# Hash attention and squared-ReLU feed-forward on one core: hash products in array quarters, key bits by Sign on ACT, one reciprocal spread by a matmul

## The chip, the core and the metric

The kernel runs on one core of a Trainium2 chip. The metric is device time in microseconds (us), the median of the runs shown. The engines are PE (TensorE), DVE (VectorE), ACT (ScalarE), POOL (GpSimd) and SP (SyncE, which issues DMAs). Each takes its instructions in program order.

## The reference, cut

```
q, k, v: (4, 8, 768, 64)   proj: (64, 6)   w_in: (512, 2048)   w_out: (2048, 512)

q_bucket = sum over 6 bits of (q @ proj > 0) * 2^bit          # k_bucket likewise
scores   = q @ k^T / 8, set to -1e9 where q_bucket != k_bucket
attn     = exp(scores - max) / (sum + 1e-9)
x        = (attn @ v), heads side by side: (3072, 512)
h        = x @ w_in ;  r = max(h, 0) ;  out = (r * r) @ w_out
```

## The kernel before, in words

**First stage, attention.** Heads are handled in 16 pairs (`pr`), two heads on the 128 partitions, 64 each. A pair has 768 queries and 768 keys, and is walked in six steps (`kt`), one for each 128 keys. The loop runs over `u`, the number of the step over all pairs, and an engine's instructions stand in the order in which the loop writes them.

- `features(pr, w, r)` (w = 0 queries, 1 keys; r = half of the 768): three PE transposes into a PSUM bank `tp` (L232), copied by ACT to `feat` (L237).
- `hash_bits(pr, w, r)`: one product of 384 columns with `projs[w]`, a 128x128 matrix holding `proj` for both heads (L244, tile `hp`), and one DVE instruction that makes of it the numbers `bits` in bf16 (L247): compare with `bars`, multiply by `gains`. Query bits and key bits are made such that their product is zero where all six bits agree and hugely negative elsewhere.
- `score(pr, kt)`: bits product and feature product of both heads add up in PSUM tiles `st` (L274). The two tiles of a step take four banks, and there are no others: a step's score waits for the exp of the step before. ACT then makes `e` = exp of it (L281), one instruction for each head.
- `attend(pr, kt)`: `e` times `v` into tile `xo` (L306), two steps behind the score. There is one `xo`: the first attend of a pair waits until the pair before has been normalized.
- `add_up(pr, kt)`: DVE adds the `e` of the step into `total` (L295), one step behind the score.
- `sum_up(pr)`: once a pair, `total` summed over keys by four PE products with ones (L320, tile `tot`), a DVE transpose (`flip`), one small addition (`once`), eight reciprocals of 32 partitions that copy the result to where both halves of the queries need it (`rec`, L336), and a DVE transpose that spreads it (`recs`, L340). `normalize(pr)` multiplies `xo` by `recs` into `x_t` (L350).
- `PREPARE` says which parts of the next pair's features and bits are made in which step.
- The weights come as 64-bit floats and are turned into 32-bit ones beside the attention, 32 pieces, one every third step (`load_weight`, `part_weight`, `round_weight`). For a piece DVE cuts out exponent and mantissa (L127, L131), POOL scales the exponent (L136, L139), ACT makes `one` of the mantissa (L142); a step later DVE rounds (L152, L156) and POOL multiplies (L159). Two pieces fall on a pair: `part_weight` at kt 0 and kt 3, `round_weight` at kt 1 and kt 4.

In a step of the loop before, the order is: score, the totals of a pair that is done, attend, normalize, PREPARE, add_up, weights.

**Second stage, feed-forward.** Six chunks of 512 tokens: `hid` (L453), ReLU on ACT, square on DVE, `y` (L470), out.

PSUM has eight banks: four for `st`, two for `xo`, two that `tp`, `hp` and `tot` take in turn (`bank`).

Of the kernel before, what the change touches and what calls it, by code (L numbers as in the profile page):

```python
# [33 lines left out]
def kernel(  # L34
# [131 lines left out]

    projs, bars, gains = [], [], []
    for w, name in ((0, "q"), (1, "k")):  # L170
        projs.append(const.tile([P, P], FP32, name=f"proj_{name}"))
        bars.append(const.tile([P, 1], FP32, name=f"bar_{name}"))
        gains.append(const.tile([P, 1], FP32, name=f"gain_{name}"))
    pj = const.tile([P, NBITS], FP32, name="pj")
    ones = const.tile([P, 32], FP32, name="ones")
    NRING = 8
    ring = [const.tile([P, S + 1], FP32, name=f"e{i}") for i in range(NRING)]

    def constants():
        N = NBITS  # L180
        for h in range(2):
            r = h * D
            nc.gpsimd.dma_start(out=pj[r:r + D], in_=proj)
        for w in range(2):
            nc.gpsimd.memset(projs[w], 0.0)
            nc.vector.memset(bars[w], 0.0)
            nc.vector.memset(gains[w], float(w == 0))
        for h in range(2):
            r = h * D
            nc.vector.memset(bars[0][r:r + 2 * N], -1.0)  # L190
            nc.vector.memset(bars[0][r:r + N], 0.0)
            nc.vector.memset(bars[1][r:r + N], -1.0)
            nc.vector.memset(gains[1][r:r + 3 * N], 2.0 * FAR)
            nc.vector.memset(gains[1][r:r + 2 * N], -FAR)
            for w, at in ((0, 0), (0, 2 * N), (1, N), (1, 2 * N)):
                nc.vector.tensor_copy(
                    out=projs[w][r:r + D, r + at:r + at + N], in_=pj[r:r + D]
                )
        nc.vector.memset(ones, 1.0)
        for e in ring:  # L200
            nc.vector.memset(e[:, S:S + 1], TINY)

# [33 lines left out]
            )  # L236
        nc.scalar.copy(out=feat[pr, w][:, r * HS:(r + 1) * HS], in_=tp[:, 0:HS])  # L237

    def hash_bits(pr, w, r):
        if r == 0:  # L240
            bits[pr, w] = p_f.tile([P, S], BF16, name=f"bits{w}")
        cut = slice(r * HS, (r + 1) * HS)
        hp = bank("hp")
        nc.tensor.matmul(  # L244
            out=hp[:, 0:HS], lhsT=projs[w], rhs=feat[pr, w][:, cut], start=True, stop=True
        )
        nc.vector.tensor_scalar(  # L247
            out=bits[pr, w][:, cut], in0=hp[:, 0:HS], scalar1=bars[w], scalar2=gains[w],
            op0=ALU.is_gt, op1=ALU.mult,
        )  # L250


    PREPARE = (
        ((features, 0, 0), (features, 0, 1)),
        ((features, 1, 0),),
        ((features, 1, 1), (hash_bits, 0, 0)),
        ((hash_bits, 0, 1),),
        ((hash_bits, 1, 0),),
        ((hash_bits, 1, 1),),
    )  # L260

    weights = {}
# [36 lines left out]
    def attend(pr, kt):  # L299
# [3 lines left out]
        for c in range(2):  # L303
            n = HS + c
            for h in range(2):
# [4 lines left out]
                    start=(kt == 0), stop=(kt == SB - 1),  # L310
                )

    def sum_up(pr):


# [10 lines left out]
        NB = HS // 32  # L326
        once = p_n.tile([P, NB], FP32, name="once")
        nc.vector.tensor_scalar(
            out=once, in0=flip.rearrange("p (n f) -> p n f", f=32)[:, :, 0],
            scalar1=S * TINY, scalar2=None, op0=ALU.add,  # L330
        )
        rec = p_n.tile([P, 2, NB], FP32, name="rec")
        for g in range(4):
            for c in range(2):
                at = 64 * (g // 2) + 32 * c
                nc.vector.reciprocal(  # L336
                    out=rec[g * 32:(g + 1) * 32, c], in_=once[at:at + 32]
                )
        recs[pr] = p_n.tile([P, S], FP32, name="recs")
        nc.vector.transpose(  # L340
            out=recs[pr].rearrange("p (n f) -> p n f", f=32),
            in_=rec.rearrange("p c (n o) -> p (c n) o", o=1).to_broadcast([P, S // 32, 32]),
        )

    def normalize(pr):
# [14 lines left out]
    with tc.manual_schedule():  # L360
# [5 lines left out]
        for w in range(2):  # L366
            for r in range(2):
                features(0, w, r)
            for r in range(2):
                hash_bits(0, w, r)  # L370
# [299 lines left out]
```

## Time and profile before

| | us |
|---|---|
| median of 3 runs | 1123.32 (1123.3 to 1124.17) |
| the profiled execution | 1123.84 |
| its span | 1122.1 |
| PE busy | 1067.4 |
| DVE, ACT, POOL busy | 418.7, 265.2, 88.6 |
| first score (L274) of the loop starts | 14.22 |
| first matmul of the second stage (L453) starts | 455.49 |

The span runs from the first to the last instruction of one profiled execution; its own time lies 1.74 us above it. Granted TensorE clock over the span: 0.998. In the profile a matmul of 32-bit floats leaves two records, one for each pass, so "x2" behind a hash product is one product. A row of the chain of waits shows what the end of the span hung on at that time. "issue" there is time for which the profile shows no releaser.

### The profile page before, as it was taken

To read this page: it belongs to the slowest core of one execution; us is meant where nothing else is said; L and a number is where in the kernel's file an instruction comes from. 1 tells how busy PE (TensorE), PEld (TensorE's weight loads), DVE (VectorE), ACT (ScalarE), POOL (GpSimd) and SP (SyncE) were. 2 spreads that over 40 slices of the span, in tenths; PEclk is the share of its full clock that TensorE was granted. 3 is DMA by queue.
4 is the path that set the end of the run, shared out by engine and by line. 5 is a ranking of instruction groups with operands and counts; after the bars stand their busy time and mean duration, and the time that the engine had idled before them with its cause. 6 is when DMAs were issued, how large, how long until landed. Compare 5 with 4: busy or idle time off the path is not lost.

```text
span 1122.1 us, 9897 instructions
## 1 busy us (share of the span) xinstructions
PE 1067.4 (95%) x3906; PEld 466.6 (42%) x3906; DVE 418.7 (37%) x707; ACT 265.2 (24%) x409; POOL 88.6 (8%) x106
## 2 busy tenths in 40 slices
PE   6999999999999998999999999999999999999998
PEld 3333333333333333444444444444444444444443
DVE  2777777777777778520034103400120012001100
ACT  3444444444444444210011001100110011001100
POOL 0111111111111112100000000000000000000000
PEclk9999999999999999999999999999999999999999
DMA  8233333332222111000042004200000000000000
GB/s 192 67 82 83 83 82 82 83 81 80 81 80 80 52 38 38 1 1 9 19 146 88 9 19 150 85 9 19 9 1 9 19 9 1 19 20 0 1 19 21
DMA packets 65012, 55.24 MB, mean 49 GB/s; under 512 B 51648, under 2 KB 55744, under 8 KB 64960
## 3 DMA queue, kind: packets, MB, share of 16 engines
q1 hardware_dynamic: 63328, 54.14, 16.7%
q8 instruction: 33, 0.54, 0.2%
q10 hardware_dynamic: 1568, 0.39, 0.2%
q14 instruction: 19, 0.16, 0.0%
q0 software_dynamic: 64, 0.00, 0.0%
HBM read 48.24 MB, written 6.29 MB: 49 GB/s over the span
## 4 chain that ended last, share of the span: by engine, by line
PE 89%; DVE 4%; issue 4%; ACT 2%; DMA 0%; SPq 0%; ACTq 0%; DVEq 0%
PE hid L453 29%; PE y L470 29%; PE st L274 13%; PE xo L306 11%; PE hp L244 3%; DVE total L295 2%; PE tp L232 2%; ACT e L281 2%; PE tot L320 1%; DVE power L127 1%; DVE one L131 1%; DMA q_nat<-in_q_dram 0%; DVE bits L247 0%; DVE gate L461 0%; SPq L219 0%
## 5 line engine op out<-in xcount | busy, mean ns | idle before, releaser
L453 PE MATMUL hid<-x_t,w_in 128*128 128x512 f32 x768 | 330.8, 592 | 0.0
L470 PE MATMUL y<-w_out,gate 128*128 128x512 f32 x768 | 330.6, 592 | 0.0
L461 DVE TENSOR_TENSOR gate<-r 128x512 f32<-128x512 f32 x96 | 66.5, 693 | 506.3 <-ACT r L459 504.9
L470 PEld LDWEIGHTS y<-w_out,gate 128*128 128x128 f32 x768 | 145.9, 190 | 183.7 <-issue 183.4
L453 PEld LDWEIGHTS hid<-x_t,w_in 128*128 128x128 f32 x768 | 145.8, 190 | 183.4 <-issue 182.7
L281 ACT ACTIVATE e<-st 128x768 f32<-128x768 f32 x192 | 145.0, 807 | 132.3 <-PE st L274 132.3
L306 PE MATMUL xo<-e,v_nat 128*64 128x384 f32 (+1 forms) x768 | 146.2, 502 | 22.6 <-issue 22.6
L274 PE MATMUL st<-feat,feat 64*128 64x384 f32 x768 | 158.5, 486 | 0.0
L459 ACT ACTIVATE r<-hid 128x512 f32<-128x512 f32 x96 | 57.3, 597 | 275.9 <-PE hid L453 275.9
L295 DVE TENSOR_TENSOR total<-total,e 128x768 f32<-128x768 f32 x128 | 116.9, 965 | 0.0
L306 PEld LDWEIGHTS xo<-e,v_nat 128*64 128x64 f32 x768 | 48.2, 136 | 110.5 <-issue 107.9
L475 ACT COPY o<-y 128x512 f32<-128x512 f32 x24 | 14.1, 586 | 315.7 <-PE y L470 315.7
L274 PE MATMUL st<-bits,bits 64*128 64x384 bf16 x384 | 70.6, 327 | 18.2 <-ACT e L281 18.0
L274 PEld LDWEIGHTS st<-feat,feat 64*128 64x128 f32 x768 | 69.6, 189 | 31.5 <-issue 31.4
L274 PEld LDWEIGHTS <-bits 64*128 64x128 bf16 x384 | 21.0, 93 | 65.2 <-issue 52.8
L247 DVE TENSOR_SCALAR bits<-hp,bar_q,gain_q 128x384 bf16<-128x384 f32 x32 | 21.7, 677 | 60.2 <-PE hp L244 60.2
L237 ACT COPY feat<-tp 128x384 f32<-128x384 f32 x64 | 29.2, 481 | 55.6 <-PE tp L232 55.6
L136 POOL TENSOR_SCALAR power<-power 128x512 uint32<-128x512 uint32 x32 | 23.9, 748 | 211.0 <-DVE power L127 211.0
L142 ACT ACTIVATE one<-one 128x512 f32<-128x512 uint32 x32 | 20.1, 629 | 70.8 <-DVE one L131 70.7
L247 DVE TENSOR_SCALAR bits<-hp,bar_k,gain_k 128x384 bf16<-128x384 f32 x32 | 21.7, 677 | 40.1 <-PE hp L244 40.1
L295 DVE TENSOR_TENSOR total<-e,e 128x768 f32<-128x768 f32 x32 | 30.2, 984 | 0.0
L244 PE MATMUL hp<-feat,proj_k 128*128 128x384 f32 x64 | 28.9, 536 | 0.0
(50 smaller groups left out, 365.1 us busy)
## 6 DMA issues: line engine op xcount, KB each, us to landing
raw<-in_moe_w_in_dram SPq DMA_DIRECT2D x16, 512.0 KB, 4.3
raw<-in_moe_w_out_dram SPq DMA_DIRECT2D x16, 512.0 KB, 3.6
q_nat<-in_q_dram SPq DMA_DIRECT2D x32, 192.0 KB, 4.6
v_nat<-in_v_dram SPq DMA_DIRECT2D x16, 384.0 KB, 3.3
out_dram<-o SPq DMA_DIRECT2D x24, 256.0 KB, 2.0
raw_qk<-in_q_dram SPq DMA_DIRECT2D x8, 768.0 KB, 4.3
raw_qk<-in_k_dram SPq DMA_DIRECT2D x8, 768.0 KB, 4.3
k_nat<-in_k_dram SPq DMA_DIRECT2D x30, 192.0 KB, 4.6
```

Source lines behind the costliest of these rows:

```text
L136: nc.gpsimd.tensor_scalar(out=power, in0=power, scalar1=1151.0, scalar2=896.0, op0=ALU.min, op1=ALU.max,)
L237: nc.scalar.copy(out=feat[pr, w][:, r * HS:(r + 1) * HS], in_=tp[:, 0:HS])
L244: nc.tensor.matmul(out=hp[:, 0:HS], lhsT=projs[w], rhs=feat[pr, w][:, cut], start=True, stop=True)
L247: nc.vector.tensor_scalar(out=bits[pr, w][:, cut], in0=hp[:, 0:HS], scalar1=bars[w], scalar2=gains[w], op0=ALU.is_gt, op1=ALU.mult,)
L274: nc.tensor.matmul(out=st[h][:, c, 0:HS], lhsT=src[pr, 1][rows, key], rhs=src[pr, 0][rows, cut], start=first, stop=not first,)
L281: nc.scalar.activation(out=e[:, 0:S].rearrange("p (c f) -> p c f", c=2), in_=st[h][:, :, 0:HS], func=ACTF.Exp, scale=scale,)
L295: nc.vector.tensor_tensor(out=totals[pr, h], in0=in0, in1=weights[pr, kt, h][:, 0:S], op=ALU.add)
L306: nc.tensor.matmul(out=xo[h * D:(h + 1) * D, c, 0:n], lhsT=nat[pr][2][:, h, kt * D:(kt + 1) * D], rhs=weights[pr, kt, h][:, c * HS:c * HS ...
L453: nc.tensor.matmul(out=hp, lhsT=w_in[:, ft, ff * P:(ff + 1) * P], rhs=x_t[:, ft, i * NCH:(i + 1) * NCH], start=(ft == 0), stop=(ft == NFT ...
L459: nc.scalar.activation(out=r, in_=hp, func=ACTF.Relu)
L461: nc.vector.tensor_tensor(out=g, in0=r, in1=r, op=ALU.mult)
L470: nc.tensor.matmul(out=y, lhsT=gates[ff][:, n * P:(n + 1) * P], rhs=w_out[:, ff], start=(ff == 0), stop=(ff == NFF - 1),)
```

## The change

Parts of it:

1. `hash_bits` makes both halves of a side (w) at once. `projs[w]` is now 64 columns wide. Four products, each 64 rows by 64 columns of the array, take the four combinations of head and half: bank `near` gets half 0 of head 0 (partitions 0 to 63) and of head 1 (64 to 127), bank `far` gets half 1 with the heads swapped.
2. Query bits are made on DVE as before, from `near` in one instruction and from `far` in two of 64 partitions. Key bits are made on ACT with Sign, in the same three parts. `bars`, `gains` and `lifts` (the bias of Sign) hold new numbers, so that a product is still zero only where all bits agree.
3. `sum_up` takes one reciprocal of all partitions. A new function `spread` copies it to its places by two matmuls of 12 columns with the 0/1 matrices `picks` (made by eight POOL copies at the start), into unused columns of `tot`, and DVE transposes from there.
4. `sum_up` runs beside the attend of the last but one step of its pair (kt 0 of the next pair), `spread` a step later.
5. In a step `add_up` now comes first, and PREPARE comes between score and attend. PREPARE has one entry for each step; the first features of the next but one pair are made at kt 5.
6. Ahead of the loop the first pair's bits are made in two `st` tiles.

```diff
-    projs, bars, gains = [], [], []
-    for w, name in ((0, "q"), (1, "k")):
-        projs.append(const.tile([P, P], FP32, name=f"proj_{name}"))
...
+    HUGE, SMALL = 2.0**64, 2.0**-70
+    projs = [const.tile([P, D], FP32, name=f"proj_{name}") for name in "qk"]
...
+    picks = const.tile([P, 2, P], FP32, name="picks")
...
-    def hash_bits(pr, w, r):
...
+    def hash_bits(pr, w, tiles=None):
+        t = p_f.tile([P, S], BF16, name=f"bits{w}")
+        bits[pr, w] = t
+        near, far = tiles or (bank("near"), bank("far"))
+        for c, hp in ((0, near), (1, far)):
+            for h in range(2):
+                rows = slice(h * D, (h + 1) * D)
+                at = (h ^ c) * D
+                nc.tensor.matmul(
+                    out=hp[at:at + D, 0:HS], lhsT=projs[w][rows],
+                    rhs=feat[pr, w][rows, c * HS:(c + 1) * HS], start=True, stop=True,
+                )
+        def turn(out, in_, at):
+            if w == 0:
+                nc.vector.tensor_scalar(
+                    out=out, in0=in_, scalar1=bars[at], scalar2=gains[at],
+                    op0=ALU.is_gt, op1=ALU.mult,
+                )
+            else:
+                nc.scalar.activation(
+                    out=out, in_=in_, func=ACTF.Sign, scale=HUGE, bias=lifts[at]
+                )
+        turn(t[:, 0:HS], near[:, 0:HS], slice(0, P))
+        for h in range(2):
+            at = (h ^ 1) * D
+            turn(t[h * D:(h + 1) * D, HS:S], far[at:at + D, 0:HS], slice(at, at + D))

     PREPARE = (
-        ((features, 0, 0), (features, 0, 1)),
...
+        (1, features, 0, 1),
+        (1, features, 1, 0),
+        (1, features, 1, 1),
+        (1, hash_bits, 0),
+        (1, hash_bits, 1),
+        (2, features, 0, 0),
     )
...
-        rec = p_n.tile([P, 2, NB], FP32, name="rec")
-        for g in range(4):
-            for c in range(2):
-                at = 64 * (g // 2) + 32 * c
-                nc.vector.reciprocal(
-                    out=rec[g * 32:(g + 1) * 32, c], in_=once[at:at + 32]
-                )
+        nc.vector.reciprocal(out=once, in_=once)
+        onces[pr] = once, tot
+
+    def spread(pr):
+        once, tot = onces.pop(pr)
+        rec = tot[:, HS:HS + 2 * NB]
+        for c in range(2):
+            nc.tensor.matmul(
+                out=rec[:, c * NB:(c + 1) * NB], lhsT=picks[:, c], rhs=once, start=True, stop=True
+            )
         recs[pr] = p_n.tile([P, S], FP32, name="recs")
         nc.vector.transpose(...)
...
         for u in range(len(steps) + 2):
+            if 1 <= u <= len(steps):
+                add_up(*steps[u - 1])
             if u < len(steps):
                 pr, kt = steps[u]
                 if kt == 0 and pr + AHEAD < NP:
                     load_pair(pr + AHEAD, nc.sync)
                 score(pr, kt)
             done = steps[u - 2] if u >= 2 else None
+            if done is not None and done[1] == SB - 1:
+                spread(done[0])
+            if u < len(steps):
+                ahead, f, *args = PREPARE[kt]
+                if pr + ahead < NP:
+                    f(pr + ahead, *args)
             if done is not None:
-                if done[1] == SB - 1:
+                if done[1] == SB - 2:
                     sum_up(done[0])
                 attend(*done)
                 if done[1] == SB - 1:
                     normalize(done[0])
-            if u < len(steps) and pr + 1 < NP:
-                for f, w, r in PREPARE[kt]:
-                    f(pr + 1, w, r)
-            if 1 <= u <= len(steps):
-                add_up(*steps[u - 1])
```

How the instructions stand on the engines, in the order of the program. First PE, from a score to the next at kt 3 and kt 4. The first list is before, where a hash product of half a side (`hp`) follows attend:

```order
L274 MATMUL st<-bits_277,bits_329 128x384
L274 MATMUL st<-feat_222,feat_247 128x384 x2
L306 MATMUL xo<-e_101,v_nat 64x384
L306 MATMUL xo<-e_102,v_nat 64x384
L306 MATMUL xo<-e_101,v_nat 64x385
L306 MATMUL xo<-e_102,v_nat 64x385
L244 MATMUL hp<-feat_443,proj_k 128x384
L274 LDWEIGHTS bits_329
```

The second is the changed kernel at kt 3 (L302 is score, L259 hash product, L334 attend):

```order
L302 MATMUL st<-bits_303,bits_340 128x384
L302 MATMUL st<-feat_212,feat_259 128x384 x2
L259 MATMUL near<-feat_371,proj_q 64x384 x2
L259 MATMUL far<-feat_371,proj_q 64x384 x2
L334 MATMUL xo<-e_107,v_nat 64x384
L334 MATMUL xo<-e_108,v_nat 64x384
L334 MATMUL xo<-e_107,v_nat 64x385
L334 MATMUL xo<-e_108,v_nat 64x385
L302 LDWEIGHTS bits_340
```

The hash products moved between score and attend, and four quarters of both halves stand where one half stood.

Then PE at the totals. In the changed kernel they stand at kt 0, between the transposes and the attend of the last but one step:

```order
L302 MATMUL st<-feat_212,feat_259 128x384 x2
L242 MATMUL tp<-ident,q_nat 128x128 x3
L351 MATMUL tot<-total_245,ones 32x384
L351 MATMUL tot<-total_246,ones 32x384
L351 MATMUL tot<-total_245,ones 32x384
L351 MATMUL tot<-total_246,ones 32x384
L334 MATMUL xo<-e_101,v_nat 64x384
```

and the spread a step later, at kt 1:

```order
L302 MATMUL st<-feat_212,feat_259 128x384 x2
L370 MATMUL tot<-once,picks 128x12 x2
L242 MATMUL tp<-ident,k_nat 128x128 x3
L334 MATMUL xo<-e_103,v_nat 64x384
L334 MATMUL xo<-e_104,v_nat 64x384
```

Before, the totals stood at kt 1, ahead of the attend of the last step, and all that follows from them on DVE stood behind them in that same step.

Last DVE from kt 3 to kt 4, before:

```order
L247 TENSOR_SCALAR bits_476<-hp,bar_q,gain_q 128x384
L295 TENSOR_TENSOR total_449<-total_449,e_101 128x768
L295 TENSOR_TENSOR total_450<-total_450,e_102 128x768
L127 TENSOR_SCALAR power<-raw 128x512
L131 TENSOR_SCALAR one<-raw 128x512
L247 TENSOR_SCALAR bits_528<-hp,bar_k,gain_k 128x384
L295 TENSOR_TENSOR total_449<-total_449,e_103 128x768
L295 TENSOR_TENSOR total_450<-total_450,e_104 128x768
L152 SCALAR_TENSOR_TENSOR power<-raw,power 128x512
L156 SCALAR_TENSOR_TENSOR one<-raw,one 128x512
```

and in the changed kernel (L323 is the sum, L266 the query bits):

```order
L323 TENSOR_TENSOR total_431<-total_431,e_101 128x768
L323 TENSOR_TENSOR total_432<-total_432,e_102 128x768
L266 TENSOR_SCALAR bits_502<-near,bars,gains 128x384
L266 TENSOR_SCALAR bits_502<-far,bars,gains 64x384 x2
L127 TENSOR_SCALAR power<-raw 128x512
L131 TENSOR_SCALAR one<-raw 128x512
L323 TENSOR_TENSOR total_431<-total_431,e_103 128x768
L323 TENSOR_TENSOR total_432<-total_432,e_104 128x768
L152 SCALAR_TENSOR_TENSOR power<-raw,power 128x512
L156 SCALAR_TENSOR_TENSOR one<-raw,one 128x512
```

The sums now come ahead of the bits of their step. All query bits stand together at kt 3, ahead of the weight piece's cut, and the key bits have left this engine. No bits stand any more between a step's rounding (L152, L156) and the next sums.

More of the change, by code (lines that the diff above doesn't have):

```diff
@@ L201, in constants @@
             nc.vector.memset(e[:, S:S + 1], TINY)
+        for g in range(4):
+            for c in range(2):
+                at = 64 * (g // 2) + 32 * c
+                nc.gpsimd.tensor_copy(
+                    out=picks[:, c, g * 32:(g + 1) * 32], in_=ident[:, at:at + 32]
+                )
     nat, feat, bits = {}, {}, {}
@@ L311, in attend @@
                 )
+    NB = HS // 32
+    onces = {}
     def sum_up(pr):
@@ L325, in sum_up @@
         nc.vector.transpose(out=flip, in_=tot[:, 0:HS])
-        NB = HS // 32
         once = p_n.tile([P, NB], FP32, name="once")
@@ L341, in sum_up @@
             out=recs[pr].rearrange("p (n f) -> p n f", f=32),
-            in_=rec.rearrange("p c (n o) -> p (c n) o", o=1).to_broadcast([P, S // 32, 32]),
+            in_=rec.rearrange("p (n o) -> p n o", o=1).to_broadcast([P, S // 32, 32]),
         )
@@ L368 @@
                 features(0, w, r)
-            for r in range(2):
-                hash_bits(0, w, r)
+        for w in range(2):
+            st = ps_s.tile([P, 2, 512], FP32, name="st")
+            hash_bits(0, w, (st[:, 0], st[:, 1]))
+        features(1, 0, 0)
         for u in range(len(steps) + 2):
+            if 1 <= u <= len(steps):
+                add_up(*steps[u - 1])
             if u < len(steps):
```

45 lines of the change are left out of this document (16 added, 29 removed).

## The prediction

> **What bounds the kernel now.** I read the busy time by engine first, then stretches of the span, then the chain of waits through one pair of heads, then the order of time on VectorE and GpSimd there.
>
> ```profile
> span 1122.1 us, 9897 instructions
> PE 1067.4 (95%) x3906; PEld 466.6 (42%) x3906; DVE 418.7 (37%) x707; ACT 265.2 (24%) x409; POOL 88.6 (8%) x106
> ...
> core 0: us, PE busy (x) PEld busy (x) DVE busy (x) ACT busy (x) POOL busy (x), PEclk, DMA share, GB/s
> ...
> 44.34:72.08 27.74, 25.14 (x150) 10.75 (x148) 20.01 (x35) 12.04 (x18) 5.29 (x7) 1.00 0.31 82
> 99.83:432.25 332.42, 301.13 (x1772) 128.50 (x1771) 240.00 (x420) 143.16 (x214) 62.87 (x72) 1.00 0.28 77
> 455.49:1105.00 649.51, 647.93 (x1513) 286.85 (x1512) 98.69 (x128) 70.81 (x119) 1.26 (x1) 1.00 0.09 29
> ```
>
> The stretches are cut at the first matmul of each pair's totals (tile tot). One pair takes 27.74 us, and the twelve from 99.83 to 432.25 take 27.70 each. PE is busy 25.14 of them, DVE 20.01, ACT 12.04. The second stage, from 455.49, is PE from end to end (647.93 of 649.51), and the change leaves it alone. So only the attention stage can move, by what one pair takes on PE's path:
>
> ```profile
> 205.21 1.72 PE st L274 x12
> 206.93 1.44 PE xo L306 x8
> 208.37 0.80 PE tp L232 x6
> 209.17 1.72 PE st L274 x12
> 210.90 0.78 PE tot L320 x8
> 211.68 1.44 PE xo L306 x8
> 213.12 0.48 PE tp L232 x3
> 213.60 1.77 PE st L274 x12
> 215.37 1.42 issue
> 216.79 1.51 PE xo L306 x8
> 218.30 0.48 PE tp L232 x3
> 218.78 0.65 PE hp L244 x2
> 219.43 1.72 PE st L274 x12
> ...
> 222.59 0.86 PE hp L244 x2
> ...
> 225.88 0.46 DVE power L127
> 226.34 0.40 DVE one L131
> ...
> 226.82 0.04 ACT one L142
> ...
> 227.36 1.50 ACT e L281 x2
> ...
> 228.91 1.77 PE st L274 x11
> ...
> 232.12 0.84 PE hp L244 x2
> 232.96 1.72 PE st L274 x12
> ```
>
> A row is start, length, engine, tile, line. A pair is six steps (kt 0 at 205.21 to kt 5), each a score (st, 1.72) and an attend (xo, 1.44): 6 x 3.16 = 18.96. Between them lie the transposes (0.80 + 0.48 + 0.48 = 1.76), the totals (0.78) and four hash products (0.65 + 0.86 + 0.84, the fourth taken as 0.84: 3.19). That makes 24.69. Two waits make up the rest. At 215.37 PE stands 1.42 until the previous pair is normalized and its output bank free. From 223.45, where the score of kt 4 begins (222.59 + 0.86), to that of kt 5 at 228.91 lie 5.46 us for 4.00 of work (1.72 + 1.44 + 0.84). The wait of 1.46 is an exp that starts late: ACT's copy "one" of a weight piece stands in front of it, and waits for DVE (226.34), which was behind the sums. 24.69 + 1.42 + 1.46 = 27.57; the rest is score and attend rows of 1.77 and 1.51 behind a wait.
>
> **The change, part by part, per pair.** The other prices come from these rows:
>
> ```profile
> 205.84 3.56 DVE L295 TENSOR_TENSOR total<-total,e 128x768 f32<-128x768 f32 x4
> ...
> 212.57 1.84 DVE L336 RECIPROCAL rec<-once 32x12 f32<-32x12 f32 x8
> 214.45 0.98 DVE L340 STREAM_TRANSPOSE recs<-rec 128x768 f32<-128x768 f32 x1
> 215.54 1.15 DVE L350 SCALAR_TENSOR_TENSOR x_t<-xo,recs 128x384 f32<-128x384 f32 x2
> 216.61 0.68 DVE L152 SCALAR_TENSOR_TENSOR power<-raw,power 128x512 uint32<-128x512 uint32 x1
> ...
> 231.25 1.27 POOL L159 TENSOR_TENSOR w_in<-one,power 128x512 f32<-128x512 f32 x1 [3.35 <-DVE one L156]
> ```
> ```profile
> 439.24 2.89 DVE L295 TENSOR_TENSOR total<-e,e 128x768 f32<-128x768 f32 x2
> 439.40 1.91 POOL L159 TENSOR_TENSOR w_out<-one,power 128x512 f32<-128x512 f32 x1 [6.20 <-DVE one L156]
> ```
> ```profile
> L237 ACT COPY feat<-tp 128x384 f32<-128x384 f32 x64 | 29.2, 481 | 55.6 <-PE tp L232 55.6
> ...
> L136 POOL TENSOR_SCALAR power<-power 128x512 uint32<-128x512 uint32 x32 | 23.9, 748 | 211.0 <-DVE power L127 211.0
> ...
> L247 DVE TENSOR_SCALAR bits<-hp,bar_q,gain_q 128x384 bf16<-128x384 f32 x32 | 21.7, 677 | 60.2 <-PE hp L244 60.2
> ...
> L139 POOL TENSOR_SCALAR power<-power 128x512 uint32<-128x512 uint32 x32 | 20.4, 637 | 2.6
> ...
> L237 ACT ACT_TABLE_LOAD x1 | 1.3, 1283 | 2.1 <-issue 2.1
> ```
>
> *Hash products.* Four full-array products of 384 columns go; two groups of four 64x64 quarters come, each 384 columns and two passes like the product removed. No row shows row and column parts of the array at work together. Low end: 0.65, one full-array product with no change of shape ahead of it. High end: four in turn, 4 x 0.78 = 3.1. I take 0.78, the totals row, where four column parts with different moving data ran at once over the same 384 columns; the score's two heads likewise run beside each other on row parts. 2 x 0.78 = 1.56 against 3.19: saves 1.63.
>
> The Trainium skill speaks against it: "TensorEngine Tiling (Array Packing)", Gotcha 1: PSUM Pressure, says that different row tiles cannot access one PSUM bank at the same time. Bank near takes one quarter from each row half, and so does far. By that page the group would go two and two, the second rival; no row here shows such a pair, and the score keeps its heads in separate banks.
>
> *Transposes.* Four groups of 3 (4 x 0.48 = 1.92) for 6 + 3 + 3 (1.76): costs 0.16.
>
> *Spread.* Two matmuls of 12 columns with 128x128 weights, four passes ahead of the transposes of kt 1. Nearest rows: 0.80 for six 128x128 transposes is 0.13 a piece, so four are 0.5. Ends: nothing, and 0.8. Costs 0.5. On DVE seven reciprocals of 0.23 go.
>
> *The wait at normalization (1.42).* The totals, their transpose and the reciprocal move a step ahead; behind the spread at kt 1 stand only one transpose (0.98) and the normalization itself (1.15). The attend that needs the bank comes a score and a transpose group (1.72 + 0.48 = 2.20) behind the one that feeds normalization, so 1.15 fits, and the 0.98 lies beside the transposes and attend in front. Saves 1.42.
>
> *Key bits on ACT.* Three Sign instructions, priced as copies (0.48 each) behind the exps of kt 4. ACT is busy 12.04 of 27.74, so they hide. If Sign wanted a table of its own there would be two loads of 1.28 a pair; the row shows one load, and the changed program also has just one. Cost 0.
>
> *Query bits, and what becomes late.* On DVE three instructions (half the partitions take as long as all) replace two, all in kt 3. I count DVE from the end of the attend that feeds normalization (t = 0, the score of kt 2 begins). Normalize to 1.1, the two weight roundings (0.6 to 0.7 each) to 2.4, sums of kt 1 (2 x 0.89) to 4.2. These sums now follow directly on a rounding, which releases GpSimd's product L159. In the last pair that neighbourhood is seen: two sums took 2.89 in place of 1.78, the product 1.91 in place of 1.27. So 1.1 more: 5.3. Sums of kt 2: 7.1; bits, 3 x 0.62 (0.68 less the overlap of neighbours): 9.0; L127 and L131: 9.8; "one" on ACT ends near 10.4. On PE kt 2 takes 3.64 (1.72 + 0.48 + 1.44), kt 3 3.94, and the score of kt 4 ends at 9.3. Its exps wait until 10.4 and end at 11.9, while PE reaches the score of kt 5 at 11.5: a wait of about 0.5. Then DVE: sums of kt 3, partly against GpSimd's scaling of "power" (2.2, of which 0.4 is an estimate from the rows of L136 and L139), roundings (1.3), sums of kt 4 beside the next L159 (2.9), sums of kt 5 (1.8): 9.8 + 8.2 = 18.0. PE wants them for the totals at 11.9 + 3.64 + 1.72 + 0.48 = 17.7: with the hand-over about 0.5 more. New waits: 1.0. The ends are 0, if GpSimd and DVE miss each other, and 2.2 (third rival).
>
> *Loads, GpSimd, start.* Loads keep their order on the sync queue. The next but one pair's first queries are read at kt 5, a step early, and landed more than a pair before. Eight small copies on GpSimd run before the loop. Cost 0.
>
> Sum per pair: 18.96 + 1.56 + 1.92 + 0.78 + 0.50 + 1.0 = 24.7 against 27.7 to 27.75: saves 3.0. Fourteen pairs: 42. The first pair has both hash groups and one late exp but no normalization wait: 2.5. The start may win half a microsecond. The last pair has no hash work and now waits for its own sums before the totals; between +2 and -2, taken as 0. In all 45.
>
> The profiled execution took 1123.84 (span 1122.1 and 1.74 around it), 0.52 over the median of the runs, 1123.32. 1123.84 - 45 = 1078.8; as a median 1078.
>
> **The rivals.**
> - *DVE is in time.* For it: DVE has 20.01 - 1.6 - 0.7 = 17.7 us of work in 24.7. Against: its order. Without the two waits 23.7 a pair, 14 x 1.0 less: 1064.
> - *The quarters go two and two.* Each group 1.56 in place of 0.78; of the 1.56 per pair about 1.0 fills the time PE would wait for DVE anyway: +0.6 a pair, 1087.
> - *GpSimd holds DVE back more.* Both scalings of both weight pieces could meet sums, 2 x (0.75 + 0.64) = 2.8 where 0.4 is counted. DVE itself waits for PE at kt 0 and kt 1, which I guess takes up half of the 2.4: +1.2 a pair, 1095. The Trainium skill, "SBUF — State Buffer", section "SBUF: two separate sides", calls the shared port an exclusive lock, held for a whole instruction, for a VectorE instruction with two SBUF inputs against a GpSimd one. The 2.89 above agrees; that page gives the direction of this rival, not its size.
> - *Slower.* The quarters run in turn, each with its own change of shape: 2 x 3.1 a pair. DVE is then never late: 18.96 + 6.2 + 1.92 + 0.78 + 0.5 = 28.4, 0.65 over now: 14 x 0.65 = 9, about 1132. It decides from 2.8 per group upward. Against it: totals and score overlap their parts.
>
> **How the numbers follow.** Forecast, 1070 to 1083: 50%. DVE in time (1058 to 1070): 18%. Two and two, or more from GpSimd (1083 to 1100): 24%. Both with some further wait (1100 to 1121): 4%. No change that can be told from the measurement's 0.2%: 1%. Slower: 3%. The range 1060 to 1098 leaves out some 14%. Faster 96%, same 1%, slower 3%.
>
> **What would show it.** A pair of 24.7 between first totals matmuls. The four quarters within 0.8, not 1.5. No idle time of PE ahead of attend at kt 2. PE waiting for ACT's exp at kt 5 and for the sums at the totals, about 0.5 each; sums on DVE and GpSimd's L159 with longer means than now. One table load. I am wrong if the quarters do not overlap, if a wait for DVE appears at the spread, or if the second stage changes by more than a microsecond.

## The result, and the profile after

The changed kernel took 1076.87 us, median of four runs (1076.36 to 1077.34), against 1123.31 for the kernel before (1123.02 to 1124.17): ratio 0.9585, 95% interval 0.9569 to 0.9602. Forecast was 1078.0. The profiled execution took 1077.06, with a span of 1075.2. First the head of its page, then busy time by stretches (the columns are those of the prediction's stretches): about one pair of heads (24.40 of its 24.49), the last pair from its first score on, and the second stage.

```profile
span 1075.2 us, 10208 instructions
PE 1055.7 (98%) x4098; PEld 460.4 (43%) x4098; DVE 424.2 (39%) x577; ACT 286.6 (27%) x457; POOL 116.1 (11%) x114
```
```profile
37.60:62.00 24.40, 24.34 (x162) 10.46 (x162) 20.52 (x28) 13.51 (x22) 7.09 (x6) 1.00 0.35 92
...
377.53:408.59 31.06, 28.87 (x162) 11.37 (x161) 24.31 (x33) 11.14 (x16) 8.85 (x9) 0.95 0.09 31
408.59:1058.00 649.41, 647.83 (x1513) 286.82 (x1512) 96.28 (x120) 70.77 (x119) 1.26 (x1) 1.00 0.09 29
```

PE's share of the span rose from 95% to 98%. The second stage is the same work in the same time: it begins at 408.59 in place of 455.49, 46.90 earlier, and all that the change did lies ahead of it. A pair's DVE time did not fall (20.52 in that stretch, against 20.01 for a pair of before) though reciprocals and key bits left DVE: its sums became longer, as shown below.

Between first totals matmuls, pairs 2 to 13 now take 24.49 each; they took 27.75. The chain of waits through one such pair, from the score of kt 0 to the next totals:

```profile
182.14 1.72 PE st L302 x12
183.86 0.48 PE tp L242 x3
184.34 1.16 PE tot L351 x8
185.50 1.44 PE xo L334 x8
186.94 1.72 PE st L302 x12
188.66 0.55 PE tot L370 x4
189.21 0.38 PE tp L242 x3
189.58 1.47 PE xo L334 x8
...
200.00 0.43 DVE power L127
200.43 0.35 DVE one L131
...
200.85 0.04 ACT one L142
...
201.39 1.50 ACT e L309 x2
...
202.93 1.77 PE st L302 x11
204.71 0.48 PE tp L242 x3
205.18 1.44 PE xo L334 x8
206.63 1.72 PE st L302 x12
208.35 0.48 PE tp L242 x3
208.82 1.16 PE tot L351 x8
```

Three things are to be seen. The 1.42 ahead of an attend is gone. The totals take 1.16 where their work is 0.78: 0.38 of it is a wait for the sums, which the row carries inside its length. In the trace behind the row at 208.82 one of the four products starts at 208.75 and the other three at 209.14, when the last sum has ended (209.09). And between 189.58 and 202.93 the chain leaves PE for DVE, L142 and the late exp, as it did before; but PE now loses little there (0.38 to 0.40 ahead of the score at 202.93, where it lost 1.46). The spread costs 0.55 + 0.38 + 1.47 for spread, transposes and attend, against 0.48 + 1.44: 0.48 net. PE's timeline at the query's hash products:

```profile
196.32 0.54 PE L259 MATMUL near<-feat,proj_q 64*64 64x384 f32 x2
196.33 0.54 PE L259 MATMUL far<-feat,proj_q 64*64 64x384 f32 x2
196.69 0.49 PE L259 MATMUL near<-feat,proj_q 64*64 64x384 f32 x2
196.70 0.49 PE L259 MATMUL far<-feat,proj_q 64*64 64x384 f32 x2
197.12 1.51 PE L334 MATMUL xo<-e,v_nat 128*64 128x384 f32 x8
```

All four quarters run side by side. A row here joins records of both heads: the first records of the four products start at 196.317, 196.323, 196.330 and 196.337, and the attend follows 0.80 after the first. Work of a pair is thus 18.96 + 2 x 0.80 + 1.92 + 0.78 + 0.48 = 23.74, and two waits of 0.38 make 24.50, against 24.49 measured.

DVE's order of time in this pair, and GpSimd's beside it:

```profile
193.34 2.90 DVE L323 TENSOR_TENSOR total<-e,e 128x768 f32<-128x768 f32 x2
...
200.68 2.65 DVE L323 TENSOR_TENSOR total<-total,e 128x768 f32<-128x768 f32 x2
...
204.45 4.64 DVE L323 TENSOR_TENSOR total<-total,e 128x768 f32<-128x768 f32 x4
```
```profile
193.51 1.91 POOL L159 TENSOR_TENSOR w_in<-one,power 128x512 f32<-128x512 f32 x1 [5.03 <-DVE one L156]
...
201.32 1.20 POOL L139 TENSOR_SCALAR power<-power 128x512 uint32<-128x512 uint32 x1
204.61 1.92 POOL L159 TENSOR_TENSOR w_in<-one,power 128x512 f32<-128x512 f32 x1 [2.09 <-DVE one L156]
```

The last DVE row holds two pairs of sums, the first of them beside GpSimd's L159. Each pair of sums that a GpSimd instruction runs into takes 2.65 to 2.9 in place of 1.8, and GpSimd's takes longer too (L159 1.92 for 1.27). Over the kernel (groups by line: count, busy time, mean ns, idle time before), followed by ACT's Sign and its table loads:

```profile
L323 DVE TENSOR_TENSOR total<-total,e 128x768 f32<-128x768 f32 x128 | 145.6, 1186 | 1.5 <-ACT e L309 1.5
L323 DVE TENSOR_TENSOR total<-e,e 128x768 f32<-128x768 f32 x32 | 45.3, 1456 | 6.3 <-ACT e L309 6.3
```
```profile
L271 ACT ACTIVATE bits<-far,lifts 64x384 bf16<-64x384 f32 x30 | 17.3, 575 | 0.6
...
L247 ACT ACT_TABLE_LOAD x1 | 1.3, 1283 | 2.1 <-issue 2.1
```

There is one table load, so Sign needs no table of its own. The last pair, from its first score to the second stage, went against the change: 31.06, where it had taken 28.39. Its rows on PE:

```profile
401.88 2.23 PE L351 MATMUL tot<-total,ones 128*32 128x384 f32 x8 [1.94 <-DVE total L323]
404.04 2.63 PE L334 MATMUL xo<-e,v_nat 128*64 128x384 f32 x8
```

PE waits 1.94 for the last sums, and then the granted clock is at half from 402.93 for 3.41 us, so that totals take 2.23 and an attend 2.63. The run with the cutting ahead (among the experiments) has the same wait there, and the clock stays up:

```profile
399.78 1.71 PE L351 MATMUL tot<-total,ones 128*32 128x384 f32 x8 [1.94 <-DVE total L323]
```

From its last score (kt 5) to the second stage that run takes 10.46, the changed kernel 12.11. So the half clock costs 1.65 here; with the clock up the last pair would have taken about 29.4, an estimate from these two. The kernel before also has a spell of 3.41 in its last pair, from 438.38, behind its normalization wait:

```profile
438.22 2.72 PE L306 MATMUL xo<-e,v_nat 128*64 128x384 f32 x8 [1.96 <-issue]
```

But its last totals stood behind two attends that PE could run while DVE finished, and from its last score to the second stage it took 7.58.

The sum: pairs -46.29 (fourteen, from the first score of the second pair to that of the last), first pair -2.34 (from its first score to that of the second), start -0.94 (first score at 13.28, was 14.22), last pair +2.67: together -46.90.

### The profile page after: what moved, and what is told of

Same layout as the page of the kernel before. It is cut to its first block, busy times and chain, and to the rows that moved or that the text cites. A ratio compares the mean times of both kernels' runs of the same rounds, so it can differ in the third digit from the quotient of the medians.

```text
span 1075.2 us, 10208 instructions
## 1 busy us (share of the span) xinstructions
PE 1055.7 (98%) x4098; PEld 460.4 (43%) x4098; DVE 424.2 (39%) x577; ACT 286.6 (27%) x457; POOL 116.1 (11%) x114
## 4 chain that ended last, share of the span: by engine, by line
PE 82%; DVE 9%; issue 6%; ACT 2%; DMA 0%; SPq 0%; ACTq 0%
PE hid L492 31%; PE y L509 31%; PE st L302 8%; PE xo L334 7%; DVE total L323 2%; PE tp L242 2%; ACT e L309 2%; PE tot L351 2%; DVE bits L266 2%; DVE x_t L384 1%; DVE one L156 1%; PE tot L370 1%; DVE power L152 1%; DVE power L127 1%; DMA q_nat<-in_q_dram 0%
## 5 line engine op out<-in xcount | busy, mean ns | idle before, releaser
L302 PE MATMUL st<-feat,feat 64*128 64x384 f32 x768 | 158.3, 485 | 0.0
L334 PE MATMUL xo<-e,v_nat 128*64 128x384 f32 (+1 forms) x768 | 146.4, 503 | 0.0
L323 DVE TENSOR_TENSOR total<-total,e 128x768 f32<-128x768 f32 x128 | 145.6, 1186 | 1.5 <-ACT e L309 1.5
L302 PEld LDWEIGHTS st<-feat,feat 64*128 64x128 f32 x768 | 69.3, 188 | 26.9 <-issue 26.4
L334 PEld LDWEIGHTS xo<-e,v_nat 128*64 128x64 f32 x768 | 46.8, 137 | 73.3 <-issue 73.2
L302 PE MATMUL st<-bits,bits 64*128 64x384 bf16 x384 | 70.7, 327 | 3.6 <-ACT e L309 1.5
L302 PEld LDWEIGHTS <-bits 64*128 64x128 bf16 x384 | 19.8, 93 | 69.9 <-issue 56.2
L323 DVE TENSOR_TENSOR total<-e,e 128x768 f32<-128x768 f32 x32 | 45.3, 1456 | 6.3 <-ACT e L309 6.3
L136 POOL TENSOR_SCALAR power<-power 128x512 uint32<-128x512 uint32 x32 | 22.9, 717 | 180.1 <-DVE power L127 180.1
L142 ACT ACTIVATE one<-one 128x512 f32<-128x512 uint32 x32 | 20.2, 630 | 73.3 <-DVE one L131 73.3
L159 POOL TENSOR_TENSOR w_in<-one,power 128x512 f32<-128x512 f32 x16 | 30.7, 1918 | 56.9 <-DVE one L156 56.9
L159 POOL TENSOR_TENSOR w_out<-one,power 128x512 f32<-128x512 f32 x16 | 30.0, 1876 | 55.9 <-DVE one L156 55.9
L139 POOL TENSOR_SCALAR power<-power 128x512 uint32<-128x512 uint32 x32 | 29.1, 910 | 2.6
```

The costliest lines, as they stand in the source:

```text
L136: nc.gpsimd.tensor_scalar(out=power, in0=power, scalar1=1151.0, scalar2=896.0, op0=ALU.min, op1=ALU.max,)
L139: nc.gpsimd.tensor_scalar(out=power, in0=power, scalar1=-896.0, scalar2=2.0**23, op0=ALU.add, op1=ALU.mult,)
L159: nc.gpsimd.tensor_tensor(out=pieces[i][3], in0=one, in1=power.bitcast(FP32), op=ALU.mult)
L302: nc.tensor.matmul(out=st[h][:, c, 0:HS], lhsT=src[pr, 1][rows, key], rhs=src[pr, 0][rows, cut], start=first, stop=not first,)
L323: nc.vector.tensor_tensor(out=totals[pr, h], in0=in0, in1=weights[pr, kt, h][:, 0:S], op=ALU.add)
L334: nc.tensor.matmul(out=xo[h * D:(h + 1) * D, c, 0:n], lhsT=nat[pr][2][:, h, kt * D:(kt + 1) * D], rhs=weights[pr, kt, h][:, c * HS:c * HS ...
```

## Experiments

My theory: PE's time per pair is its work plus two short waits, and both waits are DVE's lateness, made by the order of its work and by sums that meet GpSimd. Diffs are against the changed kernel, except where the text names another.

**Hash products alone.** The kernel before, with only the quarters and Sign. Totals, reciprocals and the order inside a step (sums last, PREPARE behind attend) go back to what they were:

```diff
-        nc.vector.reciprocal(out=once, in_=once)
-        onces[pr] = once, tot
+        rec = p_n.tile([P, 2, NB], FP32, name="rec")
+        for g in range(4):
+            for c in range(2):
+                at = 64 * (g // 2) + 32 * c
+                nc.vector.reciprocal(
+                    out=rec[g * 32:(g + 1) * 32, c], in_=once[at:at + 32]
+                )
...
-                if done[1] == SB - 2:
+                if done[1] == SB - 1:
                     sum_up(done[0])
...
+            if 1 <= u <= len(steps):
+                add_up(*steps[u - 1])
```

> The kernel before with the quarter hash products and Sign on ACT alone: totals, eight reciprocals and the order inside a step as before (hash products behind attend, sums behind them). Theory (the gain comes from the two parts together, and DVE's order decides): the products save 1.6 us of PE per pair, but three instructions for the query bits now stand on DVE at kt 3 in front of the sums, the weight piece's cut and ACT's copy, so the exp of kt 4 comes about 1.5 later than before; the 1.42 wait for normalization stays. About 27.8 us per pair, no change: 1119 to 1126. Rival (terms add up, PE's work is what counts): 27.75 - 1.6 = 26.1 per pair, about 1098.

Measured: 1134.52 (1133.37 to 1135.68), ratio 1.0094, interval 1.0065 to 1.0123. A pair takes 27.81 where the clock stays up, as the theory had it: 1.6 less work on PE, and nothing won. PE's rows at kt 5:

```profile
208.47 0.32 PE L302 MATMUL st<-bits,bits 64*128 64x384 bf16 x1 [2.15 <-ACT e L309]
...
209.17 0.32 PE L302 MATMUL st<-bits,bits 64*128 64x384 bf16 x1 [0.38 <-ACT e L309]
```

The wait at the score of kt 5 shows as 2.15 + 0.38 of idle time. From the score of kt 4, at 202.28, to the row at 209.17 lie 6.89 us for 3.96 of work: a wait of 2.93 by the measure by which it was 1.46. So the exp came about 1.5 later, as the theory had it, and this takes back what the hash products save. The wait at normalization (1.48) stays. The time was over the upper end of what I expected by 8 us, and this I had not foreseen: in seven spells of the attention stage, 27.3 us in all, the granted clock was at half, and five pairs took 29.2 to 30.5.

**Totals alone.** The other half: one reciprocal, the spread, the early totals and the early sums stay, the hash products and both kinds of bits go back to the old form, and PREPARE stands behind attend again.

```diff
+        hp = bank("hp")
+        nc.tensor.matmul(
+            out=hp[:, 0:HS], lhsT=projs[w], rhs=feat[pr, w][:, cut], start=True, stop=True
+        )
+        nc.vector.tensor_scalar(
+            out=bits[pr, w][:, cut], in0=hp[:, 0:HS], scalar1=bars[w], scalar2=gains[w],
+            op0=ALU.is_gt, op1=ALU.mult,
+        )
...
+        ((1, features, 1, 1), (1, hash_bits, 0, 0)),
+        ((1, hash_bits, 0, 1),),
+        ((1, hash_bits, 1, 0),),
+        ((1, hash_bits, 1, 1), (2, features, 0, 0)),
```

> The kernel before with the totals alone changed: one reciprocal, spread by two matmuls, totals a step earlier, sums first in the step; full-array hash products in four steps behind attend as before (the first features of the next but one pair at kt 5, to fit the banks). Theory: the normalization wait of 1.42 goes, spread costs 0.5, the late exp behind the weight piece's cut stays in part: about 26.5 per pair, 1103 to 1109. Together with the run without a gain from the hash part, the parts alone would then give 1.3 of the 3.26 that both give. Rival (terms add up): 3.26 less 1.6 for the hash products, so 26.1 per pair, about 1100.

Measured: 1104.34, ratio 0.9825, interval 0.9797 to 0.9854; 26.37 per pair, as expected. The totals now wait for sums (a row of 1.71 with 0.19 idle ahead of it, for 0.78 of work). So the parts alone bring 0 and 1.38 per pair, and together 3.26. It is not the normalization wait that keeps the hash products' saving from showing: the run with the old totals, below, has that wait too.

**Two full-array products in place of four quarters.** The bits of a side then take two instructions in place of three; everything else is as in the changed kernel.

```diff
-            for h in range(2):
-                rows = slice(h * D, (h + 1) * D)
-                at = (h ^ c) * D
-                nc.tensor.matmul(
-                    out=hp[at:at + D, 0:HS], lhsT=projs[w][rows],
-                    rhs=feat[pr, w][rows, c * HS:(c + 1) * HS], start=True, stop=True,
-                )
+            nc.tensor.matmul(
+                out=hp[:, 0:HS], lhsT=projs[w],
+                rhs=feat[pr, w][:, c * HS:(c + 1) * HS], start=True, stop=True,
+            )
```

> The changed kernel with each group of four quarters replaced by two full-array products (both halves of a side, one after the other); bits then in two instructions instead of three. PE work per pair grows by 2 x (1.45 - 0.80) = 1.3. Theory (PE would otherwise wait for DVE, so most of it fills waits): 24.8 to 25.0 per pair in place of 24.49, about 1082 to 1086. Rival (PE's work adds in full): 25.8, about 1096.

Measured: 1085.70, ratio 0.9659, interval 0.9631 to 0.9687; 25.10 per pair, 0.1 over the theory and far from the rival. About half of the added PE work is seen (0.61); the other half fills time in which PE had waited for DVE. DVE also has one instruction of about 0.7 less ahead of the sums here, and the run does not tell the two apart.

**The old totals.** The changed kernel with eight reciprocals and totals at kt 1.

```diff
-                if done[1] == SB - 2:
+                if done[1] == SB - 1:
                     sum_up(done[0])
```

> The changed kernel with the totals as before: at kt 1, eight reciprocals, no spread; all else as changed. Theory: the wait for normalization at kt 2 comes back (1.4 or somewhat more, DVE being fuller), the spread's 0.55 and the totals' wait of 0.38 go: 25.3 to 25.7 per pair, 1089 to 1095. Rival (the normalization wait would be hidden by the new order inside the step): 23.6 to 24.5 per pair, 1065 to 1077.

Measured: 1097.10, ratio 0.9761, interval 0.9733 to 0.9789; 26.04 per pair. The direction was right, the size was not: 0.3 to 0.7 more than expected. The chain shows the normalization wait back (first row) and a second one that I had not counted:

```profile
203.01 1.46 issue
...
211.68 0.79 PE near L259 x4
212.47 0.59 PE far L259 x4
```

The key's group takes 1.38 in place of 0.80: its far quarters start only some 0.6 later. Beside the run of the hash products alone, this one has the new order inside a step (part 5 of the change) and nothing else, and a pair is 1.77 shorter, 1.71 shorter than in the kernel before. So quarters and Sign need that order to pay; which part of the order does it was not tried.

**No work on GpSimd.** GpSimd's three instructions per weight piece are left out; the weights are set to zero once, so the output of the second stage is left out too.

```diff
-        nc.gpsimd.tensor_scalar(
-            out=power, in0=power, scalar1=1151.0, scalar2=896.0, op0=ALU.min, op1=ALU.max,
-        )
-        nc.gpsimd.tensor_scalar(
-            out=power, in0=power, scalar1=-896.0, scalar2=2.0**23, op0=ALU.add, op1=ALU.mult,
-        )
...
-        nc.gpsimd.tensor_tensor(
-            out=pieces[i][3], in0=one, in1=power.bitcast(FP32), op=ALU.mult
-        )
...
+        nc.gpsimd.memset(w_in, 0.0)
+        nc.gpsimd.memset(w_out, 0.0)
```

> The changed kernel without GpSimd's three instructions per weight piece; DVE's and ACT's parts of the conversion stay. w_in and w_out are set to zero once, so the output is left out. Theory (the new waits of 0.40 and 0.38 come from sums that GpSimd's instructions hold back): sums at 0.95 again, both waits gone, 23.6 to 23.7 per pair, attention 13 us shorter; with the last pair's wait for its sums shorter too about 1061 to 1064. Rival (the waits come from the amount and order of DVE's own work): 24.2 to 24.5 per pair, 1072 to 1077.

Per pair this hit: 23.73, both waits gone. The sums' group in this run:

```profile
L314 DVE TENSOR_TENSOR total<-total,e 128x768 f32<-128x768 f32 x128 | 116.7, 955 | 7.1 <-ACT e L300 7.1
```

955 ns a sum against 1186: GpSimd is what makes them long. The time did not hit: 1072.97 (ratio 0.9549, interval 0.9529 to 0.9568), 9 us over the upper end, because the two memsets ahead of the loop (6.9 each on GpSimd; DVE's small copies of `proj` beside them end at 17.8) put the first score off from 13.28 to 21.70 and the first totals from 37.6 to 48.1. The per-pair number stands, the total tells nothing.

**Key bits on DVE.** Three tensor_scalar on DVE in place of three Sign on ACT.

```diff
-                nc.scalar.activation(
-                    out=out, in_=in_, func=ACTF.Sign, scale=HUGE, bias=lifts[at]
+                nc.vector.tensor_scalar(
+                    out=out, in0=in_, scalar1=kbars[at], scalar2=0.5,
+                    op0=ALU.is_gt, op1=ALU.subtract,
                 )
```

> The changed kernel with the key bits on DVE (three compares at kt 4, numbers chosen so that the mask is the same) and no Sign on ACT. DVE gains 2.0 us of work per pair at kt 4, between the sums and the totals that wait for it. Theory (DVE decides the new waits): nearly all of it appears at the totals, 26.0 to 26.6 per pair, 1099 to 1110. Rival (DVE has room, 18 of 24.5 us; or ACT's lateness decides): 24.0 to 24.6 per pair, 1070 to 1079.

Measured: 1113.46 (1111.93 to 1114.98), ratio 0.9909, interval 0.9889 to 0.9929; 25.5 to 26.75 per pair (28.1 in one at half clock). Of 22.6 us at half clock, 10.2 lie in the first pair, 10.2 in three spells of the last pairs, and the rest at the very end. The rival is out, the theory's time was a few us short. PE at the totals:

```profile
200.81 1.62 PE L352 MATMUL tot<-total,ones 128*32 128x384 f32 x8 [1.74 <-DVE total L324]
```

Two microseconds more on DVE come back as 1.74 of waiting at the totals, and as a longer row (1.62 for 0.78). ACT carries the same three for nothing. With the rest of the change in place, the place of the key bits is worth 36.6 us; between the two traces 26.9 of it lie in the fourteen pairs, the rest at both ends, partly at half clock.

**DVE's order.** The same instructions as the changed kernel; the rounding of a weight piece goes ahead of the spread's transpose at kt 1, where DVE waits for PE, and the cutting of the next piece ahead of the query bits at kt 3.

```diff
+            if u % SB == 1 and 0 <= i - 1 < len(pieces):
+                round_weight(i - 1)
+            if u % SB == 3 and 0 <= i - 1 < len(pieces):
+                part_weight(i - 1)
             if done is not None and done[1] == SB - 1:
                 spread(done[0])
```

> The changed kernel with two moves on DVE: at kt 1 the weight rounding goes ahead of the transpose that waits for the spread (so GpSimd's product runs beside instructions that are not held back by it), and at kt 3 the weight piece's cut goes ahead of the query bits (so ACT's copy and the exp are not late). Theory: both new waits gone, 23.7 per pair, 1062 to 1066. Rival (another bound close behind, such as ACT's chain of score and exp): 24.1 to 24.5, 1070 to 1077.

Measured: 1062.93 (1062.61 to 1063.77), ratio 0.9460, interval 0.9444 to 0.9476; 23.73 per pair, PE's work and nothing else. GpSimd does as much as in the changed kernel, so it is not its work that costs, but where it falls: L159 at kt 1 now lies beside the transpose, and the sums of kt 1 are short.

```profile
185.84 0.98 DVE L374 STREAM_TRANSPOSE recs<-tot 128x768 f32<-128x768 f32 x1
187.19 1.15 DVE L384 SCALAR_TENSOR_TENSOR x_t<-xo,recs 128x384 f32<-128x384 f32 x2 [0.37 <-PE xo L334]
188.26 1.81 DVE L323 TENSOR_TENSOR total<-e,e 128x768 f32<-128x768 f32 x2
```
```profile
186.01 1.28 POOL L159 TENSOR_TENSOR w_in<-one,power 128x512 f32<-128x512 f32 x1 [1.41 <-DVE one L156]
```

**Each move alone.** To see which move removes which wait: first the rounding at kt 1 alone. The diff is against the kernel with both moves.

```diff
-            early = u % SB in (1, 3)
+            early = u % SB == 1
...
-            if u % SB == 3 and 0 <= i - 1 < len(pieces):
-                part_weight(i - 1)
```

> The changed kernel with one of the two moves: the rounding of the weight piece (round_weight) is issued ahead of the spread's transpose at kt 1, so that GpSimd's product L159 lies beside the transpose's and normalization's wait for PE and no longer beside the sums of kt 1; the cutting of the next piece (part_weight) stays behind the query bits at kt 3. Theory (one lateness of DVE, made at kt 1, carried through kt 3 and seen by PE twice): DVE is about 1.0 us earlier from the sums of kt 1 on, so both waits of PE shrink, together from 0.78 to 0.2 or less: 23.8 to 24.0 us per pair, 1064 to 1069 us. Rival (two separate waits, that at the totals alone from this order): 0.38 goes, the wait at the score of kt 5 stays at 0.4: 24.1 to 24.2 us per pair, 1071 to 1073 us.

Measured: 1064.55 (1064.35 to 1065.14), ratio 0.9475, interval 0.9460 to 0.9491; 23.83 per pair. The theory hit, and the rival (two separate waits) is out: this one move takes 0.66 of 0.76, and what is left is 0.10 at the totals (0.88 for 0.78). The first sums of a pair (total<-e,e), those that met L159 at kt 1, are short again, 951 ns where they were 1456:

```profile
L323 DVE TENSOR_TENSOR total<-e,e 128x768 f32<-128x768 f32 x32 | 29.1, 951 | 6.3 <-ACT e L309 6.3
```

Then the cutting at kt 3 alone, against the same.

```diff
-            early = u % SB in (1, 3)
+            early = u % SB == 3
...
-            if u % SB == 1 and 0 <= i - 1 < len(pieces):
-                round_weight(i - 1)
```

> The changed kernel with the other move alone: the cutting of the weight piece (part_weight: L127, L131 on DVE, then ACT's copy one) is issued ahead of the query bits at kt 3; the rounding stays behind normalization. Theory (one lateness): ACT's copy comes 1.8 us earlier, so the exp of kt 4 is no longer behind it and the wait at the score of kt 5 goes; but the sums still meet GpSimd's product at kt 1 and kt 4, DVE reaches the sums of kt 5 as late as now, and PE, now 0.4 earlier, waits at the totals for longer, 0.4 to 0.8: 24.1 to 24.5 us per pair, 1071 to 1077 us. Rival (two separate waits): 0.4 goes in full: 24.1 or less, 1071 or less, and in both the wait ahead of the score of kt 5 is gone.

Measured: 1073.83 (1073.22 to 1074.32), ratio 0.9560, interval 0.9544 to 0.9576; 24.29 per pair. Time and size lie in the theory's range, but for another reason than it gave: the totals no longer wait at all (0.78). What is left sits at the key's hash products, on DVE and PE:

```profile
199.33 1.37 DVE L266 TENSOR_SCALAR bits<-far,bars,gains 64x384 bf16<-64x384 f32 x2
```
```profile
200.19 0.86 PE L259 MATMUL near<-feat,proj_k 64*64 64x384 f32 x4
200.76 0.86 PE L259 MATMUL far<-feat,proj_k 64*64 64x384 f32 x4
```

Far's quarters start at 200.76, 0.06 behind the end of the query bits (199.33 + 1.37 = 200.70), 0.57 behind near's. The cutting ahead of the query bits makes these late, and the key's group waits for the banks that they read. PE, held up there, comes to the totals when the sums are done. The run with the old totals shows the same: query bits end at 212.11, far's quarters start at 212.17. That the bank is what it waits for is read from this order of time and from the shared pool of banks, and was not tried by itself.

**A better tail.** The kernel with DVE's order, and in the last pair the last attends ahead of totals and spread, so that PE has work while DVE finishes. The diff is against that kernel.

```diff
-            if done is not None and done[1] == SB - 1:
+            if done is not None and done[1] == SB - 1 and u < len(steps):
                 spread(done[0])
...
-                if done[1] == SB - 2:
+                last = u >= len(steps)
+                if done[1] == SB - 2 and not last:
                     sum_up(done[0])
                 attend(*done)
+                if done[1] == SB - 2 and last:
+                    sum_up(done[0])
                 if done[1] == SB - 1:
+                    if last:
+                        spread(done[0])
                     normalize(done[0])
```

> As the run before, and for the last pair alone the attend of the last but one and of the last step stand ahead of the totals and of the spread, so that PE has work while DVE still sums. Theory: 1 to 3 us less than the run before, from the last pair (in the changed kernel PE waits 1.94 there and the granted clock halves for 3.4 us). Rival (the second stage then waits for nothing anyway, since its first chunk does not read the last pair): no difference over 0.5.

Measured: 1061.40 (1060.87 to 1062.16), ratio 0.9447, interval 0.9431 to 0.9462: 1.5 better than DVE's order alone, as expected, and the best version here, 15.5 below the changed kernel. In PE's timeline two attends (sixteen records) stand ahead of the last totals, whose row takes 0.95, where one without a wait has 0.85:

```profile
387.25 2.81 PE L334 MATMUL xo<-e,v_nat 128*64 128x384 f32 x16
389.98 0.95 PE L351 MATMUL tot<-total,ones 128*32 128x384 f32 x8
```

## Why the prediction was right

*What bounds it.* Right: the second stage did not move, and the gain is 14 pairs of PE's path. Per pair 3.26 was won where 3.0 was forecast.

*Hash products.* Forecast 0.78 a group, measured 0.80. The rival that took two and two is out: with full-array products, 1.3 more work, a pair took 25.10, and the changed kernel's rows show all four at once. The Trainium skill, "TensorEngine Tiling (Array Packing)", Gotcha 1: PSUM Pressure, says that row tiles cannot access one bank at the same time; near and far each took quarters from both row halves here, on different partitions, and the measured 0.80 decides against that rule for this case.

*Transposes, spread, normalization.* 1.92 as forecast; spread 0.48 (0.5); the 1.42 is gone, and comes back (1.46) when the totals are put back.

*Key bits on ACT.* Sign took 0.58, not the copy's 0.48, all of it hidden; one table load. Cost 0 was right, and the run with key bits on DVE shows what stood behind that zero.

*The new waits.* Forecast 0.5 at each of two places, measured 0.38 at the totals and 0.38 to 0.40 at the score of kt 5: about 0.77 in place of 1.0. Their places and their cause (sums that meet GpSimd) were right. That they are mostly one lateness and not two was seen only in the run of the rounding alone. The rival of more GpSimd collisions was right in part: at kt 3 the scaling of the weight piece makes two sums 0.85 longer (2.65), where 0.4 was counted, and L139 takes 1.20. The scaling of the piece cut at kt 0 meets no sum (its L139 takes 0.62), because DVE waits for PE then. So of the rival's 2.8 about 0.85 came, and L139's mean of 910 ns, 637 before, is that of one that meets sums and one that does not.

*What was mis-sized.* "The start may win half a microsecond": 0.94. "The last pair ... taken as 0": +2.67, outside the +2 that I gave as its bound. Up to its last score that pair takes 1.8 less than before, from there to the second stage 4.5 more: the wait for its own sums, which I had named, and 1.65 of half clock behind it, which the term left out. Without the half clock it would have been about +1.0, an estimate. The fourteen pairs won 4.3 more than their 42 (14 x 0.26, and 0.65 in those with ends of their own), the start 0.4 more, the first pair 0.2 less, the last 2.7 less: 1.9 in all, 46.9 in place of 45. These errors have opposite signs, so that the median came 1.1 us from the forecast is in part luck. With the pairs' error alone it would have been about 1074, with the last pair's alone about 1081, both within the range.

## What to carry to other kernels

A cut of work on the bounding engine pays only as far as its waits do not grow: find the wait that ends last in a pair, and remove it together with the work, since here the two parts alone brought 0 and 1.38 of 3.26. Quarters and Sign brought nothing in the old order inside a step, and 1.71 in the new one. Before taking work off an engine that feeds the bound, look at its order: placing work that keeps another engine busy where this one waits anyway was worth 14 us here with no instruction less. A row that merges several matmuls and is longer than their work (1.16 for 0.78) holds a wait, though its idle column shows nothing.

## What the runs showed of the hardware

- Quarters of 64x64 from both row halves write two banks at once, each bank from both halves on different partitions: four in 0.80, where four tiles of 32 columns for the totals take 0.78.
- Some waits of PE were followed by 3.41 us at half of the granted clock: 1.94 (changed kernel, last pair), 1.96 (before and old totals, last pair), 1.79, 2.25 and 1.95 (key bits on DVE), and 2.15 + 0.38 in some pairs of the run of hash products alone. The same waits were also followed by none: 1.94 in the last pair of the runs with the totals alone, the full-array products and the cutting ahead, 1.74 to 1.79 in most pairs of key bits on DVE, and 2.15 + 0.38 in the other pairs of hash products alone. Waits of 1.42 to 1.48 in the pairs of the kernel before and of the run with old totals had none behind them. The Trainium skill, "TensorE: Matmul & The Clock Gate", gives a free-running window of about 3.4 us; the spells' 3.41 agrees with that, and their coming and going would fit it, though no run here tests it. It puts the idle time that lowers the clock above about 3 us, which 1.79 to 1.96 here does not bear out.
- A GpSimd instruction and a sum that meet both get longer, by 0.85 to 1.1 for two sums and 0.6 for GpSimd's, and which loses can turn: with DVE's order, sums of 1.81 stood beside an L159 of 2.78.
